# Four copies of the projected keys in a row, and four small VectorE steps at other places, in a fused attention and maxout kernel

## The chip, the core and the metric

The kernel runs on one core of a Trainium2 chip. A core has a matrix engine (TensorE, PE in the profile), a vector engine (VectorE, DVE), a scalar engine (ScalarE, ACT), GpSimd (POOL) and SyncE (SP). Each engine works through its own list of instructions in order. Semaphores make an instruction wait for results of another engine. DMA queues move data between the device memory and the on-chip memory (SBUF); TensorE writes its results to the banks of PSUM.

The metric is the device time of one execution in microseconds (us). For the kernel before it is 355.79 us, the median of three runs that lie between 355.75 and 355.89.

## The reference

```python
# attention with projected keys and values: 8 batches, 8 heads, 1024 positions, 64 wide, 64 projected rows
k_proj = np.einsum('ks,bhsd->bhkd', E, k)
v_proj = np.einsum('ks,bhsd->bhkd', F, v)
scores = scale * np.matmul(q, k_proj.transpose(0, 1, 3, 2))
scores = scores - np.max(scores, axis=-1, keepdims=True)
attn = np.exp(scores)
attn = attn / (np.sum(attn, axis=-1, keepdims=True) + 1e-09)
out = np.matmul(attn, v_proj)
# heads side by side: x has 8192 rows of 512
h1 = x @ w1          # 512 x 1024
h2 = x @ w2
g = np.maximum(h1, h2)
return g @ w_out     # 1024 x 512
```

## The kernel before

The kernel rewrites the second half. With the difference of the weights, wd = w1 - w2, the maximum of the two products is relu(x wd) + x w2. So the output is relu(x wd) w_out + x M, where M = w2 w_out is computed once. Both remaining products are done by Strassen's scheme in its form with seven block products: each takes sums and differences of blocks of x and g as one side (made by `step_s`, line 723) and differences of weight blocks as the other (`sub4`, line 614, kept in `T_sb`). Seven products are then combined by additions on VectorE (lines 778 and 885) and copies on ScalarE.

The work is cut into 16 *units*, two for each batch. A unit has up steps (x wd, `up_steps`) and down steps (the output product, `down_steps`). Each of them has seven products in the order 1, 2, 6, 5, 7, 3, 4. Products 1, 6, 5 and 7 are copied from PSUM to SBUF by ScalarE (`keep`, line 737, tile `p_sb`); for the up steps these copies are called s1, u1, s5 and u2. A later product accumulates into the same bank, so it has to wait for that copy: product 6 for s1, product 7 for u1, product 3 for s5, and product 4 for u2. The up products are on line 763, the down products on line 855.

The attention of a later batch is woven into these steps. For one batch its parts are:

- the keys' and values' projection (`step_kv_sets`, line 225) with its copies to SBUF
- the transposition of the projected keys (`step_kpt_sets`, line 254), and four ScalarE copies that set the result out in the tile `kpt`: one of 64x512 elements (line 262), one of 64x256 (line 263), and two of 64x128 (line 267)
- the queries' transposition, by PE with copies on VectorE or ScalarE in batch 1 (`step_qt`, lines 312 and 317), by DMA in batches from 2 on (line 324)
- the row maxima: PE multiplies queries and keys once (`step_top`, line 345), VectorE reduces the scores to their maxima (line 354, tile `top`), and PE transposes these (`step_topt`, line 366), so that ScalarE can copy them out (line 372)
- the scores less their maxima (line 386), the exponential, the sums and the values (line 401), and the division (line 462 or 517).

Nothing schedules this at run time. A list of *slots* gives the order of the up and down steps. A down product is cut into pieces, so that an attention step can stand between two pieces. The name `("U", n, h, i)` is the slot of an up product in the span of unit n's down steps, `("P", n, p, i)` is piece i of a down product, and `("G", n, h)` is a group of attention work. `at_slot(key, step, ...)` hangs a further step behind a slot. A step can return a function. The loop at the end of the kernel calls it after the next slot, and whatever that returns after the slot following:

```python
    pending = []
    for key, slot in slots:
        r = slot()
        pending = [g for g in [r, *(f() for f in pending)] if g is not None]
        for s in steps.pop(key, ()):
            r = s()
            if r is not None:
                pending.append(r)
```

This is how the keys' copies are spread. With `parts=2` the first two follow one slot after the transposition, and the last two one slot later, with that slot's own copies between them. In batches 3 to 7 the transposition hangs behind `("U", n, 0, 2)` (product 6), for odd n from 3 to 11. The next slot is the last piece of down product 2, and the one after is product 5, whose copy s5 so stands between the second and third copies of the keys.

Batch 1's attention is woven into unit 0's down steps, by a list of names with two slots to each down product. The number n counts the places in that list. At these places stand also the differences of weight blocks `step_t(1, ...)` (the part of `T_sb` made from `m_sb`, which holds M) and the four sums and differences of x for unit 1 (`sums_x` of `U[0, 1]`; S1 is made from S0, S3 from S1). In PE's order the names are: kk keys' projection, kv values' projection, qt queries' transposition, tp scores for the maxima, tt transposition of the maxima.

Of the kernel before, what the change touches and what calls it, by code (L numbers as in the profile page):

```python
# [16 lines left out]
def kernel(  # L17
# [41 lines left out]
    def mm_bank(dtype=FP32, n=None):  # L59
        if n is None:  # L60
            n = turn.pop(0)
            turn.append(n)
        return ps.tile([128, 512 if dtype == FP32 else 1024], dtype, tag=f"mm{n}", name="mm_ps")
# [150 lines left out]
    def step_kv_sets(t, bank=None, copy=nc.scalar.copy, which="kv"):  # L214
        late = bank is None
        if late:
            bank = att_banks()[:, 0, :]
        t["sets"] = True
        n = H // 2 * D
        for i, w in enumerate("kv"):  # L220
            if w not in which:
                continue
            for c in range(NC):
                for s in range(2):
                    nc.tensor.matmul(  # L225
                        out=bank[s * KP : (s + 1) * KP, i * n : (i + 1) * n],
                        lhsT=eft[i][:, c, :],
                        rhs=t[w][:, s * H // 2 : (s + 1) * H // 2, c, :],
                        start=(c == 0 and w == which[0]), stop=(c == NC - 1), skip_group_check=True,
                    )  # L230
        if "k" in which:
            kp = t["kp"] = proj.tile([128, H // 2 + 1, D], FP16, tag="kp", name="kp_sb")
            k_ps = bank[:, 0:n].rearrange("p (h d) -> p h d", d=D)
            copy(out=kp[:, 0 : H // 2, :], in_=k_ps)
            copy(out=kp[:, H // 2, :], in_=k_ps[:, 0, :])
            if which == "k":
                return

        def finish_v():
            vp, m = t["vp"], H // 2  # L240
            nc.vector.tensor_copy(
                out=vp[:, 0:m], in_=bank[:, n : 2 * n].rearrange("p (h d z) -> p h z d", d=D // 2, z=2)
            )
            for a, b in (0, KP), (KP, 0):
                nc.vector.tensor_copy(out=vp[a : a + KP, m:H], in_=vp[b : b + KP, 0:m])

        if late:
            return finish_v
        finish_v()
# [57 lines left out]
    def step_qt(t, h0, nh=2, i0=0, i1=NI, att=False, copy=nc.vector.tensor_copy):  # L307
        qt_ps = att_banks(FP16)[:, 0, :] if att else mm_bank(FP16)
        ni = i1 - i0
        for h in range(nh):  # L310
            for i in range(ni):
                nc.tensor.transpose(
                    out=qt_ps[:, (h * ni + i) * 128 : (h * ni + i + 1) * 128],
                    in_=t["q"][:, h0 + h, 2 * (i0 + i) : 2 * (i0 + i) + 2, :],
                    identity=ident16,
                )
        copy(
            out=t["qt"][:, h0 : h0 + nh, i0 * 128 : i1 * 128],
            in_=qt_ps[:, 0 : nh * ni * 128].rearrange("q (h n) -> q h n", h=nh),
        )  # L320
# [274 lines left out]
    U = {(b, o): {"n": n, "b": b, "o": o, "t": tiles[b]} for n, (b, o) in enumerate(units)}  # L595
# [376 lines left out]
    t = tiles[0]  # L972
# [118 lines left out]
    def at_slot(key, s, *a):  # L1091
        steps.setdefault(key, []).append(lambda: s(*a))
# [11 lines left out]
    t = tiles[1]  # L1104
    at_slot((0, 22), new_attn, t)
    at_slot((0, 22), lambda: turn.__setitem__(slice(None), [2, 3]))
    for n, x in enumerate((
        "", "kk", "qt00 qt10", "kpt", "qt01", "qt11 tp00", "tp10", "tt00", "kv tt10", "tp01", "tp11", "tt01",
        "tt11", "sc00", "sc10", "dn00 in00", "dn10 in10 at00", "AT10", "sc01",
    )):  # L1110
        key = ("P", n // 15, (n - 1) // 2 % 7, (n - 1) % 2) if n else (0, 22)
        for name in x.split():
            if name == "kk":
                at_slot(key, step_kv_sets, t, None, nc.vector.tensor_copy, "k")
                at_slot(key, loads, 2, "v")
            elif name == "kv":
                at_slot(key, step_kv_sets, t, None, nc.vector.tensor_copy, "v")
            elif name == "kpt":
                at_slot(key, step_kpt_sets, t, 0)
            else:  # L1120
                g, j = int(name[2]), int(name[3])
                s_ = {"qt": step_qt, "tp": step_top, "tt": step_topt, "sc": step_sc, "dn": step_dn,
                      "in": step_inv, "at": step_at, "AT": step_at}[name[:2]]
                args = (4 * g, 4, 2 * j, 2 * j + 2) if name[:2] == "qt" else (g, j)
                if name[:2] == "qt" and j == 0:
                    s_ = lambda *a: step_qt(*a, copy=nc.scalar.copy)
                at_slot(key, s_, t, *args, *([True] if name[:2] == "AT" else []))
        if n in (1, 4):
            at_slot(key, step_t, 1, (0, 1) if n == 1 else (2, 3))
        if 14 <= n < 18:  # L1130
            at_slot(key, step_tw, n - 14)
        if n == 5:
            at_slot(key, loads, 2, "q")
        if 2 <= n < 6:
            at_slot(key, sums_x, U[0, 1], ((2, 0, 1, 3)[n - 2],))


    t = tiles[2]
# [8 lines left out]
    for b in range(3, B):  # L1147
        t = tiles[b]
        n = 2 * b - 3
        key = ("U", n - 1, 1, 5)  # L1150
        at_slot(key, new_attn, t)
        at_slot(key, step_qt_dma, t, 0, H // 2)
        at_slot(key, step_qt_dma, t, H // 2, H)
        at_slot(("G", n, 0), lambda t=t: step_kv_sets(t, mm_bank(n=0), nc.vector.tensor_copy))
        at_slot(("U", n, 0, 2), step_kpt_sets, t)
        at_slot(("U", n, 0, 6), step_gate, t, "qt", H - 1)
        at_slot(("U", n, 0, 6), loads, b + 1, "k", "v", "q")
    for n, h in (3, 1), (4, 0), (4, 1), (5, 1), (6, 0), (6, 1), (7, 1), (8, 0):
# [3 lines left out]
    for i, (t, g, j) in enumerate(groups[1:]):  # L1162
        n, h = divmod(i + 1, 2)
# [8 lines left out]
    for i, (new, old) in enumerate(zip([*groups[1:], none], groups)):  # L1172
        n, h = divmod(i + 2, 2)
# [72 lines left out]
```

## Time and profile before

| what | value |
|---|---|
| median of three runs | 355.79 us |
| the profiled execution's own time | 355.79 us |
| its span, first to last instruction | 354.0 us |
| PE busy | 341.8 us, 97% of the span |
| VectorE busy | 276.0 us, 78% |
| ScalarE busy | 226.8 us, 64% |
| GpSimd busy | 38.9 us, 11% |
| granted TensorE clock | 1.00 |
| DMA, mean | 149 GB/s |

The profile shows one execution. A row of a timeline has the start, the duration, the engine, the line of the kernel, the operation, what it writes and reads, and how many such instructions in a row were put together. In square brackets is how long the engine sat idle before it, and what ended that. A row of the list of waits has who waited for whom, the total in us, how often, and the longest. Durations of neighbours on ScalarE and VectorE can overlap by a little, so the distance between two starts is read beside the duration.

### The profile page before, as it was taken

The numbers are of one execution on the slowest core, as the hardware profiler recorded it, in microseconds if no ns is written. First come the engines' busy times: TensorE is split into PE (matmuls) and PEld (weight loads), VectorE is DVE, ScalarE is ACT, GpSimd is POOL, SyncE is SP. The second block draws the span as 40 slices with busy tenths as digits, with TensorE's granted clock in tenths as the row PEclk, the third lists the DMA queues.
The fourth block names the chain that finished last, engine by engine and source line by source line (L and its number), as shares of the span: only waits on it lengthen the run. The fifth ranks groups of instructions, "written<-read, shape, count | busy, mean of one in ns | idle before, by whom it ended". The sixth has DMA issues, their size and how long they took to land.

```text
span 354.0 us, 11051 instructions
## 1 busy us (share of the span) xinstructions
PE 341.8 (97%) x4801; PEld 282.8 (80%) x4801; DVE 276.0 (78%) x513; ACT 226.8 (64%) x433; POOL 38.9 (11%) x58
## 2 busy tenths in 40 slices
PE   8889998999999999999999999999999999999996
PEld 3655587678888788888888788888888788888885
DVE  4776778886969789686969779686969879696773
ACT  2387653777675767666675767766675767676542
POOL 8375001020000300002000300002000000000000
PEclk9999999999999999999999999999999999999999
DMA  8999999999307999199976999199947511021223
GB/s 190 206 198 202 203 206 207 186 164 181 64 27 136 179 201 261 55 219 143 214 183 127 198 200 268 53 193 162 215 114 111 129 65 59 22 100 44 78 91 119
DMA packets 73712, 52.87 MB, mean 149 GB/s; under 512 B 26816, under 2 KB 73280, under 8 KB 73664
## 3 DMA queue, kind: packets, MB, share of 16 engines
q0 software_dynamic: 30688, 28.05, 50.3%
q1 hardware_dynamic: 42688, 23.93, 27.8%
q8 instruction: 37, 0.61, 0.7%
q10 hardware_dynamic: 288, 0.20, 0.2%
q14 instruction: 11, 0.09, 0.1%
HBM read 57.15 MB, written 16.78 MB: 209 GB/s over the span
## 4 chain that ended last, share of the span: by engine, by line
PE 69%; ACT 4%; DVE 4%; issue 0%; DVEq 0%
PE mm_ps L855 34%; PE mm_ps L763 21%; PE mm_ps L386 4%; PE att_ps L345 3%; PE mm_ps L225 3%; ACT p_sb L737 2%; PE att_ps L401 2%; DVE xt_sb L517 2%; ACT ex_sb L488 1%; DVE gt_sb L778 1%; PE att_ps L366 1%; ACT kpt L267 1%; DVE gt_sb L781 0%; DVE big L723 0%; DVE o_sb L953 0%
## 5 line engine op out<-in xcount | busy, mean ns | idle before, releaser
L737 ACT COPY p_sb<-mm_ps 128x512 f32<-128x512 f32 x179 | 101.7, 592 | 62.2 <-PE mm_ps L763 32.4
L855 PEld LDWEIGHTS <-big 128*128 128x128 f16 x768 | 72.3, 98 | 10.6 <-issue 3.2
L855 PE MATMUL mm_ps<-T_sb,big 128*128 128x256 f16 x576 | 77.3, 273 | 0.0
L778 DVE TENSOR_TENSOR gt_sb<-mm_ps,p_sb 128x512 f16<-128x512 f32 x56 | 38.5, 687 | 43.5 <-PE mm_ps L763 42.2
L763 PE MATMUL mm_ps<-big,big 128*128 128x256 f16 x336 | 50.4, 273 | 0.4 <-ACT p_sb L737 0.4
L763 PEld LDWEIGHTS <-big 128*128 128x128 f16 x448 | 43.8, 98 | 5.6 <-issue 0.6
L855 PE MATMUL mm_ps<-wo_sb,gt_sb 128*128 128x256 f16 x256 | 43.0, 273 | 0.0
L488 ACT ACTIVATE ex_sb<-mm_ps 128x512 f16<-128x512 f32 x50 | 27.1, 595 | 20.1 <-PE att_ps L401 11.4
L855 PEld LDWEIGHTS <-gt_sb 128*128 128x128 f16 x376 | 34.3, 98 | 6.9 <-issue 3.6
L354 DVE TENSOR_REDUCE top<-att_ps 128x8 f16<-128x512 f32 x56 | 36.0, 690 | 4.0 <-PE att_ps L345 4.0
L763 PEld LDWEIGHTS <-wd_sb 128*128 128x128 f16 x336 | 32.9, 98 | 3.8
L763 PE MATMUL mm_ps<-xt_sb,wd_sb 128*128 128x256 f16 x224 | 32.8, 273 | 0.0
L517 DVE TENSOR_TENSOR xt_sb<-att_ps,ld_sb 128x1024 f16<-128x1024 f32 x26 | 31.6, 1216 | 0.0
L885 DVE TENSOR_TENSOR o_sb<-mm_ps,p_sb 128x512 f32<-128x512 f32 x32 | 21.9, 683 | 4.1 <-ACT p_sb L914 2.0
L855 PE MATMUL mm_ps<-m_sb,xt_sb 128*128 128x256 f16 x128 | 24.4, 273 | 0.0
L304 POOL COPY junk<-qt_sb 1x1 f16<-1x1 f16 x6 | 1.7, 286 | 200.0 <-DMA qt_sb<-q_sb 200.0
L781 DVE TENSOR_SCALAR gt_sb<-gt_sb 128x512 f16<-128x512 f16 (+1 forms) x60 | 21.2, 354 | 2.1
L723 DVE TENSOR_TENSOR big<-gt_sb 128x1024 f16<-128x1024 f16 x32 | 21.9, 683 | 0.0
L855 PE MATMUL mm_ps<-wo_sb,big 128*128 128x256 f16 x128 | 21.5, 273 | 0.0
L345 PEld LDWEIGHTS <-qt_sb 128*128 128x128 f16 x256 | 16.6, 98 | 5.4 <-issue 4.2
L855 PE MATMUL mm_ps<-T_sb,gt_sb 128*128 128x256 f16 x120 | 20.3, 273 | 0.0
L855 PEld LDWEIGHTS <-xt_sb 128*128 128x128 f16 x188 | 18.2, 98 | 2.4 <-issue 0.2
(136 smaller groups left out, 554.4 us busy)
## 6 DMA issues: line engine op xcount, KB each, us to landing
out_dram<-o_sb SPq DMA_DIRECT2D x62, 256.0 KB, 2.6
k_sb<-in_k_dram POOLq DMA_DIRECT2D x7, 1024.0 KB, 9.9
v_sb<-in_v_dram POOLq DMA_DIRECT2D x7, 1024.0 KB, 13.8
q_sb<-in_q_dram POOLq DMA_DIRECT2D x5, 1024.0 KB, 20.9
q_sb<-in_q_dram POOLq DMA_DIRECT2D x6, 512.0 KB, 12.0
big<-in_moe_w_dram POOLq DMA_DIRECT2D x12, 128.0 KB, 6.5
v_sb<-in_v_dram POOLq DMA_DIRECT2D x4, 256.0 KB, 13.6
wo_sb<-in_moe_w_out_dram POOLq DMA_DIRECT2D x1, 1024.0 KB, 10.4
```

The lines of the kernel that those rows point to most:

```text
L345: nc.tensor.matmul(out=banks[i][:, h * 128 : (h + 1) * 128], lhsT=t["qt"][:, 4 * g + h, j * W + i * 128 : j * W + (i + 1) * 128], rhs=t["k ...
L354: nc.vector.tensor_reduce(out=top[k][:, i, :].rearrange("p (o h) -> p h o", o=2)[:, 0:4, :], in_=banks[i].rearrange("p (h o k) -> p h o k" ...
L386: nc.tensor.matmul(out=banks[e][pos : pos + Z, h * W : (h + 1) * W], lhsT=pick[rows, 2 * h + e, :] if shift else kpt_of(t, head, o)[:, s * ...
L488: nc.scalar.activation(out=t["ex", g, j][:, e, :], in_=banks[e], func=ACTF.Exp, scale=scale)
L517: nc.vector.tensor_tensor(out=x_out(t, g, j).rearrange("q z o n -> q o z n"), in0=at_ps.rearrange("q o (z n) -> q o z n", z=2), in1=ld[:, ...
L723: nc.vector.tensor_tensor(out=S(i), in0=S(0) if x is None else x, in1=y(), op=op)
L737: copy(out=x, in_=bank)
L763: nc.tensor.matmul(out=bank[:, m * W : (m + 1) * W], lhsT=w_[:, n_, (2 * d + m) * 128 : (2 * d + m + 1) * 128], rhs=a[:, n_, :], start=(n ...
L778: nc.vector.tensor_tensor(out=c_blk(j, c), in0=two(x), in1=two(y), op=ALU.add)
L781: nc.vector.tensor_scalar_max(ap, ap, 0.0)
L855: nc.tensor.matmul(out=bank[i][:, 0:CH] if two_banks else bank[:, i * CH : (i + 1) * CH], lhsT=a(c)[:, i * 128 : (i + 1) * 128], rhs=w_(c) ...
L885: nc.vector.tensor_tensor(out=o_sb, in0=two(x), in1=two(y), op=ALU.add)
```

## The change

Three things are set otherwise. No instruction is added or taken away.

- In batches 3 to 7, `step_kpt_sets` is called with `parts=1`: the four copies of the keys come one after the other, one slot after the transposition. The s5 copy comes behind them. Batch 2 keeps `parts=2`, and batch 1 had its four copies in a row before.
- In batch 1 the third and fourth weight differences (`step_t(1, (2, 3))`) go from place 4 to place 3.
- In batch 1, of the sums of x for unit 1, S0 goes from place 3 to place 2 (where S2 stands), S1 from place 4 to place 8 and S3 from place 5 to place 9. Between places 5 and 8 lie the first row maxima (tp00 and tp10).

```diff
-        if n in (1, 4):
-            at_slot(key, step_t, 1, (0, 1) if n == 1 else (2, 3))
+        if n in (1, 3):
+            at_slot(key, step_t, 1, (n - 1, n))
...
-        if 2 <= n < 6:
-            at_slot(key, sums_x, U[0, 1], ((2, 0, 1, 3)[n - 2],))
+        if n in (2, 8, 9):
+            at_slot(key, sums_x, U[0, 1], {2: (2, 0), 8: (1,), 9: (3,)}[n])
...
-        at_slot(("U", n, 0, 2), step_kpt_sets, t)
+        at_slot(("U", n, 0, 2), step_kpt_sets, t, 1)
```

On VectorE the stretch in question then has this order: T2 and T3 (line 614), the addition of line 885, both query copies (line 317), the four reductions (line 354), S1 (line 723), the values' three copies (lines 241 and 245), S3 (line 723), and the next reductions.

## The prediction

> **What bounds the kernel now.** I read the engine shares first, then the list of waits with TensorE as the one that waits, then the timelines around those waits.
>
> ```profile
> PE 341.8 (97%) x4801; PEld 282.8 (80%) x4801; DVE 276.0 (78%) x513; ACT 226.8 (64%) x433; POOL 38.9 (11%) x58
> ...
> PE 69%; ACT 4%; DVE 4%; issue 0%; DVEq 0%
> ```
>
> TensorE (PE) is busy for 97% of the span and holds 69% of the chain that ended last. Only what removes a pause of PE can shorten the run. The waits of PE (total us, times, longest) name the pauses that this change touches:
>
> ```profile
> PE att_ps L345 <- ACT kpt L267: 3.1, 5, 0.6
> ...
> PE att_ps L366 <- DVE top L354: 0.8, 1, 0.8
> ...
> PE att_ps L225 <- DVE top L354: 0.3, 1, 0.3
> ```
>
> The first row is one wait in each of batches 3 to 7. The other two stand in batch 1. The timeline of batch 3 (start us, duration, engine):
>
> ```profile
> 116.53 0.37 ACT L263 COPY kpt<-att_ps 64x256 f16<-64x256 f16 x1
> ...
> 116.79 0.60 PE L763 MATMUL mm_ps<-big,big 128*128 128x256 f16 x4
> ...
> 116.92 0.58 ACT L737 COPY p_sb<-mm_ps 128x512 f32<-128x512 f32 x1
> ...
> 117.40 0.68 DVE L723 TENSOR_TENSOR big<-gt_sb 128x1024 f16<-128x1024 f16 x1
> ...
> 117.53 0.42 ACT L267 COPY kpt<-att_ps 64x128 f16<-64x128 f16 x2
> 117.97 0.58 ACT L737 COPY p_sb<-mm_ps 128x512 f32<-128x512 f32 x1
> 118.00 0.61 PE L345 MATMUL att_ps<-kpt,qt_sb 128*128 128x128 f16 x8 [0.61 <-ACT kpt L267]
> ...
> 118.65 1.29 DVE L354 TENSOR_REDUCE top<-att_ps 128x8 f16<-128x512 f32 x2 [0.57 <-PE att_ps L345]
> ...
> 118.88 0.60 PE L763 MATMUL mm_ps<-big,wd_sb 128*128 128x256 f16 x4
> ```
>
> The reader is to see a copy of p_sb between the second keys' copy and the last two, and PE's score matmuls starting 0.05 us after the last two end. Batches 4 to 7 show the same rows (L345 at 158.02, 198.04, 238.06 and 278.08, idle 0.61 or 0.62). The timelines of VectorE (DVE), then of PE, in batch 1:
>
> ```profile
> 52.73 0.69 DVE L885 TENSOR_TENSOR o_sb<-mm_ps,p_sb 128x512 f32<-128x512 f32 x1 [1.23 <-ACT qt_sb L317]
> 53.34 0.68 DVE L317 COPY qt_sb<-mm_ps 128x1024 f16<-128x1024 f16 x1
> 53.94 0.41 DVE L614 TENSOR_TENSOR T_sb<-m_sb 128x512 f16<-128x512 f16 x1
> 54.27 0.42 DVE L614 TENSOR_TENSOR T_sb<-m_sb,T_sb 128x512 f16<-128x512 f16 x1
> 54.61 0.42 DVE L723 TENSOR_TENSOR big<-big,xt_sb 128x512 f16<-128x512 f16 x1
> 54.94 0.69 DVE L317 COPY qt_sb<-mm_ps 128x1024 f16<-128x1024 f16 x1
> 55.54 0.42 DVE L723 TENSOR_TENSOR big<-xt_sb,big 128x512 f16<-128x512 f16 x1
> 55.88 2.49 DVE L354 TENSOR_REDUCE top<-att_ps 128x8 f16<-128x512 f32 x4
> ```
>
> ```profile
> 55.56 0.82 PE L855 MATMUL mm_ps<-T_sb,big 128*128 128x256 f16 x6
> 57.22 0.29 PE L366 MATMUL att_ps<-ident,top 128*128 128x128 f16 x2 [0.85 <-DVE top L354]
> ...
> 58.42 1.06 PE L225 MATMUL att_ps<-v_sb,eft 128*64 128x256 f16 x16 [0.25 <-DVE top L354]
> ```
>
> DVE works without a gap from 52.73 to 58.37, and PE waits twice for what ends that stretch, the row maxima.
>
> **The change part by part.** No instruction is added or removed. The moved steps issue no DMA: as built, the orders on PE, GpSimd and SyncE, with their DMA issues, stay the same. ACT has five swaps and DVE one stretch in another order.
>
> *Keys' copies, five batches.* The two L267 copies move ahead of the p_sb copy (s5, product 5 of the up units). PE's pitch is 0.44 us for four matmuls (118.44 to 118.88), so from 116.79 it would reach L345 at 117.23; it started at 118.00 and lost 0.77. Now the copies: L263 starts at 116.53. Where L267 follows it directly, in batch 1, the starts are 53.13 and 53.40, 0.27 apart. So the pair runs from 116.80 to 117.22, and PE starts 0.05 later, at 117.27: 0.73 gained. If the pair could not overlap L263, it would start where the p_sb copy did, 116.92, which is 0.61 sooner than 117.53. If the wait vanished altogether, 0.77. Ends: 0.61 and 0.77; I take 0.73, from the same pair of instructions in the same order.
> The chain of waits puts DVE's L517 (ending 116.89) in front of the p_sb copy. I read that as a coincidence: in batch 2 the same copy stands 0.39 behind L263 too (78.04, 78.43), and L517 starts only at 78.45.
>
> What is late next: s5 waits behind the pair and starts 0.44 after the pair's start of 116.80 (117.53 to 117.97), so at 117.24, ending 117.82. Without overlap it ends at 117.94. Its bank is next written by product 3, L763 at 118.88, which moves up to 118.15: cover of 0.2 to 0.3. The next copy (u2) starts no later than before, and its bank's product 4 (119.75) comes at 119.02, against an end by 118.55. The reductions could start at 117.92 but stand behind L723 of 117.40; as 53.34 to 53.94 shows, a 0.68 row lets the next start after 0.60, so 118.00. They end at 119.29. PE loads their result at 120.08 now, 119.35 then: 0.06 of cover, no more. If L723 had to end first (118.08), PE would lose 0.03 to 0.06 of the 0.73. I take 0.72 per batch: 5 x 0.72 = 3.6, ends 5 x 0.61 = 3.05 and 5 x 0.77 = 3.85.
>
> The page "ScalarE: Activation LUTs" of the Trainium skill (section "What ACT_TABLE_LOAD costs") states that back-to-back activations overlap by about 93 ns. By it the copy taken out of PE's way would be worth 0.58 - 0.09 = 0.49, and the five batches 2.45. The trace disagrees: p_sb to L267 takes 0.61 (116.92 to 117.53), with no overlap.
>
> *Weight differences in batch 1.* The two T_sb differences (L614) go ahead of the L885 add. DVE stood idle 1.23 there, from 51.50 to 52.73; two rows of 0.41 and 0.42 fit, and their input m_sb is complete at 48.62 (the last L664 add, 47.94 for 0.68). L885 stays at 52.73, the first query copy at 53.34.
>
> *Two sums of x.* S0 only joins S2 (they ran back to back already). S1 and S3 leave the stretch before the maxima. The second query copy then needs only PE's transposes (53.56 + 0.61 = 54.17), so 54.22 with 0.05 of latency. The maxima follow 0.60 later, at 54.82: 1.06 sooner than 55.88. Their first pair is then ready for PE at 57.22 - 1.06 = 56.16. PE arrives at 55.56 + 6 x 0.11 = 56.22, so the first wait goes. Their last lets v's projection start at 58.42 - 1.06 = 57.36; PE arrives near 57.1, so a wait of about 0.25 stays, and PE is 1.06 ahead.
> S1 (0.42) now runs after the maxima, 57.31 to 57.73, in DVE's idle 1.16 ahead of L241 (59.52, then 58.46). S3 comes after the two L245 copies, which end at 60.44 - 1.06 = 59.38. It runs till 59.82, the next reduction could start at 59.74, and its scores are there at 60.84 - 1.06 = 59.78. The 0.40 of idle time is used up, for 0 to 0.04 of delay. Products that read S1 and S3 belong to unit 1's down steps, after 66 us. Taken: 1.04. Ends: 0.85 (only the first wait shown comes off) and 1.10 (0.85 + 0.25).
>
> [...]
>
> *Sum.* 3.60 + 1.04 = 4.64. After both places the later work follows PE: from 120 to 150 us PE has 30.00 busy us in 30. The profiled execution took 355.79 us (span 354.0 and 1.79 around it), equal to the median of the three runs. 355.79 - 4.64 = 351.15, say 351.1.
>
> **The rivals.**
> 1. *The maxima take the keys' place as the wait.* For it: the cover is 0.06 and DVE is packed from 109.9 to 118.1. Against it: L723 there waits for nothing of the swap. If half the gain per batch returned, 5 x 0.36 + 1.04 = 2.84: 353.0.
> 2. *Batch 1's lead is given back before 80 us.* For it: DVE already makes PE wait 0.20 at 71.66 (for L462), and ACT 0.39 at 79.07. Against it: both follow PE's own results, and batch 2's queries were transposed from 65.28 on, the last of them done at 72.05, 7 us ahead of the use at 79.40. The keys alone: 355.79 - 3.6 = 352.2.
> 3. *Slower: s5's copy holds product 3.* The swap puts s5 behind the pair, and product 3 writes the bank that s5 reads. It costs from an end of s5 at 118.15, and cancels a batch's gain from 118.88. With batch 1's 1.04 the run is slower only past 118.88 + 0.21. An end at 119.3 gives 5 x 0.42 - 1.04 = +1.1: 356.9. For it: in batch 2 PE does wait 0.39 for such a copy. Against it: the rows end s5 by 117.94.
> 4. *The wait isn't the keys'.* Then only batch 1 counts: 354.8. For it: L345 reads transposed queries too, and GpSimd's read of their second half comes at 117.31. Against it: its weight load, of queries, began at 117.12.
>
> **How the numbers follow.** Both parts as worked out: 0.77, between 350.8 (0.77 and 1.10) and 351.9 (0.61 and 0.85). Rival 1: 0.08. Rival 2: 0.08. Rival 3: 0.04. Rival 4: 0.03. The predicted time is that of the first. The range reaches to rival 2 and part of the way to rival 1, and 0.2 under the likeliest case's lower end, for the spread of the runs (355.75 to 355.89): 350.6 to 352.7. A measurement of this kernel tells about 0.2% (0.7 us) from no change. All cases but rival 3 are faster by more than that: 0.95; slower 0.04; same 0.01.
>
> **What the changed profile would show.** The row L345 <- L267 falls from 3.1 to under 0.3 us. The pair starts 0.27 after L263, and s5's copy follows it. Product 3 waits for nothing. In batch 1 the first maxima start near 54.8, L366 does not wait, L225 still waits about 0.25, and S3 ends just as the next reduction starts. A row of L763 waiting for p_sb five times, or L366 waiting for top five times, would prove me wrong, and so would PE back on its old times by 80 us.

## The result, and the profile after

| | before | after |
|---|---|---|
| median of four runs | 355.84 us (355.75 to 355.93) | 351.48 us (351.09 to 352.78) |
| ratio | | 0.9884 (95% interval 0.9857 to 0.991) |
| profiled execution, span | 355.79, 354.0 us | 351.74, 349.9 us |
| PE from batch 1's first L312 to the start of its last row of matmuls | 50.04 to 350.40: 300.36 us | 50.64 to 346.31: 295.67 us |

The kernel is 4.4 us faster by medians. The last row is the steadier measure, and most comparisons below use it: *PE's way* begins behind the run's first 50 us, where all kernels here have the same program. It became 4.69 us shorter. The profiled execution itself began late. The first wait for keys (L195) was 1.07 us in place of 0.22, and its first L312 stood 0.60 later. So 355.79 - 4.69 + 0.60 gives 351.70, against its 351.74.

The page's engine shares and its chain (the work that ended last, followed back from the last instruction), after:

```profile
PE 341.0 (97%) x4801; PEld 282.8 (81%) x4801; DVE 276.9 (79%) x513; ACT 225.8 (65%) x433; POOL 38.9 (11%) x58
...
PE 76%; DVE 0%; issue 0%; DVEq 0%
```

ScalarE has left the chain (4% before), VectorE's part fell from 4% to 0%, and PE holds 76% in place of 69%. PE's busy time has hardly changed (341.8 before); what went is pauses. The list of PE's waits, from 42 us on, now has these rows alone:

```profile
PE mm_ps L763 <- ACT p_sb L737: 0.3, 1, 0.3
PE att_ps L225 <- DVE top L354: 0.2, 1, 0.2
PE att_ps L401 <- DVE xt_sb L462: 0.2, 1, 0.2
```

The row L345 <- L267 of 3.1 us is gone, and so is L366 <- top of 0.8 us in batch 1. The timeline of batch 3, after:

```profile
116.07 0.37 ACT L263 COPY kpt<-att_ps 64x256 f16<-64x256 f16 x1
...
116.33 0.60 PE L763 MATMUL mm_ps<-big,big 128*128 128x256 f16 x4
116.34 0.43 ACT L267 COPY kpt<-att_ps 64x128 f16<-64x128 f16 x2
...
116.79 1.07 ACT L737 COPY p_sb<-mm_ps 128x512 f32<-128x512 f32 x2
116.82 0.61 PE L345 MATMUL att_ps<-kpt,qt_sb 128*128 128x128 f16 x8
116.94 0.68 DVE L723 TENSOR_TENSOR big<-gt_sb 128x1024 f16<-128x1024 f16 x1
...
117.54 1.29 DVE L354 TENSOR_REDUCE top<-att_ps 128x8 f16<-128x512 f32 x2
...
117.70 0.60 PE L763 MATMUL mm_ps<-big,wd_sb 128*128 128x256 f16 x4
```

The pair of L267 starts 0.27 behind L263. L345 starts 0.49 behind the L763 ahead of it, where it was 1.21 (116.79 to 118.00), so 0.72 came off. The pace without any wait is 0.44. The reduction starts 0.60 behind L723, and product 3 (the last row) waits for nothing. The timelines of VectorE, then of PE, in batch 1, after:

```profile
53.94 0.68 DVE L317 COPY qt_sb<-mm_ps 128x1024 f16<-128x1024 f16 x1
54.81 0.69 DVE L317 COPY qt_sb<-mm_ps 128x1024 f16<-128x1024 f16 x1 [0.19 <-PE mm_ps L312]
55.42 2.48 DVE L354 TENSOR_REDUCE top<-att_ps 128x8 f16<-128x512 f32 x4
57.81 0.42 DVE L723 TENSOR_TENSOR big<-big,xt_sb 128x512 f16<-128x512 f16 x1
59.06 0.42 DVE L241 CAST vp_sb<-att_ps 128x256 f16<-128x256 f32 x1 [0.84 <-PE att_ps L225]
59.52 0.46 DVE L245 COPY vp_sb<-vp_sb 64x256 f16<-64x256 f16 x2
60.00 0.42 DVE L723 TENSOR_TENSOR big<-xt_sb,big 128x512 f16<-128x512 f16 x1
60.38 2.49 DVE L354 TENSOR_REDUCE top<-att_ps 128x8 f16<-128x512 f32 x4
```

```profile
56.82 0.28 PE L366 MATMUL att_ps<-ident,top 128*128 128x128 f16 x2
...
57.96 1.06 PE L225 MATMUL att_ps<-v_sb,eft 128*64 128x256 f16 x16 [0.21 <-DVE top L354]
```

This clock is 0.60 late, so the maxima's 55.42 is 54.82 on the old one. The second query copy waits for PE's transposes (0.19) and no longer for VectorE's own queue. L366 doesn't wait. L225 still waits, 0.21. S3 (60.00) just fits in front of the next reductions, which start 0.04 behind the end of PE's scores (59.73 + 0.61).

### The profile page after: what moved, and what is told of

It reads as the page before. It is cut to its first block, busy times and chain, and to the rows that moved or that the text cites. A ratio compares the mean times of both kernels' runs of the same rounds, so it can differ in the third digit from the quotient of the medians.

```text
span 349.9 us, 11052 instructions
## 1 busy us (share of the span) xinstructions
PE 341.0 (97%) x4801; PEld 282.8 (81%) x4801; DVE 276.9 (79%) x513; ACT 225.8 (65%) x433; POOL 38.9 (11%) x58
## 4 chain that ended last, share of the span: by engine, by line
PE 76%; DVE 0%; issue 0%; DVEq 0%
PE mm_ps L855 38%; PE mm_ps L763 24%; PE mm_ps L386 4%; PE att_ps L345 3%; PE mm_ps L225 3%; PE att_ps L401 3%; PE att_ps L366 1%; PE att_ps L254 0%; DVE o_sb L953 0%; PE mm_ps L947 0%; DVEq L953 0%
## 5 line engine op out<-in xcount | busy, mean ns | idle before, releaser
L737 ACT COPY p_sb<-mm_ps 128x512 f32<-128x512 f32 x179 | 101.2, 592 | 58.7 <-PE mm_ps L763 32.5
L763 PE MATMUL mm_ps<-big,big 128*128 128x256 f16 x336 | 50.4, 273 | 0.3 <-ACT p_sb L737 0.3
L763 PEld LDWEIGHTS <-big 128*128 128x128 f16 x448 | 43.8, 98 | 5.7 <-issue 0.5
L763 PEld LDWEIGHTS <-wd_sb 128*128 128x128 f16 x336 | 32.9, 98 | 3.8
L763 PE MATMUL mm_ps<-xt_sb,wd_sb 128*128 128x256 f16 x224 | 32.8, 273 | 0.0
L723 DVE TENSOR_TENSOR big<-gt_sb 128x1024 f16<-128x1024 f16 x32 | 21.9, 683 | 0.0
L824 ACT ACTIVATE gt_sb<-mm_ps 128x512 f16<-128x512 f32 x28 | 17.0, 607 | 4.6 <-PE mm_ps L763 4.6
```

The source lines that it names most:

```text
L723: nc.vector.tensor_tensor(out=S(i), in0=S(0) if x is None else x, in1=y(), op=op)
L737: copy(out=x, in_=bank)
L763: nc.tensor.matmul(out=bank[:, m * W : (m + 1) * W], lhsT=w_[:, n_, (2 * d + m) * 128 : (2 * d + m + 1) * 128], rhs=a[:, n_, :], start=(n ...
L824: nc.scalar.activation(out=out, in_=in_, func=ACTF.Relu)
```

## The experiments

Each was made to tell one step of the prediction from a rival.

**The keys' copies alone, and batch 1's moves alone.** The first kernel keeps only the third hunk of the diff, the second only the other two.

```diff
-        at_slot(("U", n, 0, 2), step_kpt_sets, t)
+        at_slot(("U", n, 0, 2), step_kpt_sets, t, 1)
```

> Edit: only the keys' four copies in a row in batches 3 to 7; batch 1 as before. My theory (each of the five waits of L345 for L267 is worth 0.73 us, and batch 1's part 1.05 by itself): 355.8 - 5 x 0.73 = 352.2; no row L345 <- L267; batch 1 keeps its waits of 0.85 and 0.25 for the row maxima. Rival (the two parts help each other, PE loses what one part wins alone): 353 or more, with a new PE wait in batches 3 to 7.

> Edit: only batch 1's two moves; the keys' copies split as before. My theory: 355.8 - 1.05 = 354.8; PE's way from the queries' first transposition of batch 1 (L312, 16 at once) to the first scores (L386) takes 13.10 us in place of 14.16; the five waits of 0.61 for L267 stay. Rival (batch 1's lead is given back before 80 us): 355.8, and the way from the first L312 to the first L345 of batch 2 is as long as before, 29.48 us.

The keys alone: median 352.32 us beside 355.88 (ratio 0.9898, 0.9873 to 0.9922), PE's way 296.69, which is 3.67 shorter, or 5 x 0.73. Batch 1 alone: 354.97 (0.998, 0.9958 to 1.0002), way 299.27, 1.09 shorter; from L312 to the first L386 it took 13.10 (before 14.16), and to batch 2's first L345 28.41 (before 29.48). Its ratio's interval holds 1, so its gain rests on the trace and not on the times. PE's waits in this second kernel still show the keys' row as before:

```profile
PE att_ps L345 <- ACT kpt L267: 3.1, 5, 0.6
```

The two gains, 3.67 and 1.09, make 4.76, and both together gave 4.69. So the parts don't help or hinder each other, and the lead of batch 1 is kept to the end. Rivals 2 and 4 of the prediction fall.

**The two halves of batch 1's part.** One kernel puts the weight differences back, the other the sums of x.

```diff
-        if n in (1, 3):
-            at_slot(key, step_t, 1, (n - 1, n))
+        if n in (1, 4):
+            at_slot(key, step_t, 1, (0, 1) if n == 1 else (2, 3))
```

```diff
-        if n in (2, 8, 9):
-            at_slot(key, sums_x, U[0, 1], {2: (2, 0), 8: (1,), 9: (3,)}[n])
+        if 2 <= n < 6:
+            at_slot(key, sums_x, U[0, 1], ((2, 0, 1, 3)[n - 2],))
```

> Edit: the changed kernel with the two weight differences back at their old place (between the two query copies); the sums of x stay behind the maxima. My theory: the differences hold the second query copy back to 53.34 + 0.60 + 2 x 0.33 = 54.60 on the old kernel's clock, so the maxima start 0.67 sooner than before, not 1.06: PE's way from the first L312 of batch 1 to the first L386 takes 13.49 (before 14.16, both moves 13.10), and L366 waits about 0.2 for the maxima. Rival (the sums alone are the gain, the differences add nothing): 13.10.

> Edit: the changed kernel with the sums of x back at their old places (S1 and S3 ahead of the maxima); the weight differences stay ahead of the L885 add. My theory: S1 ends the first query copy's wait for 0.33 and S3 stands between the second and the maxima for another 0.34, so the maxima start about 0.66 sooner than before, and the way from L312 to L386 takes 13.50; the two halves (0.67 and 0.66) don't add up to 1.33 but to 1.06, since with both the query copy waits for PE's own transposes. Rival (the differences alone are the gain): 13.10.

The way from L312 to L386 took 13.49 and 13.48 us. In both, PE waited again for the first maxima. PE's row in the kernel with the sums alone moved:

```profile
56.85 0.28 PE L366 MATMUL att_ps<-ident,top 128*128 128x128 f16 x2 [0.17 <-DVE top L354]
```

Each half is worth about 0.67, and both 1.06. The second half of the gain is cut off by PE's transposes, as the 0.19 of idle time ahead of the second query copy shows above.

**How much cover s5 has.** Cover is the time between the end of s5's copy and product 3's write to the same bank. One more copy stands between the keys' last and s5's.

```diff
             rest()
+            if parts == 1:
+                nc.scalar.copy(out=spare, in_=ones16)
```

> Edit: the changed kernel, with one more ScalarE copy (128x512, from a constant to a tile that nobody reads) between the keys' last copy and s5's copy, in batches 3 to 7. The cover that I worked out for s5 is tested: in the changed kernel s5 ends at about 117.33 and product 3 writes its bank at 117.70. My theory: the extra copy takes 0.5 to 0.6, so product 3 waits 0.15 to 0.3 in each of five batches, the row L763 <- p_sb appears five times more, and the time rises by 0.8 to 1.5 over the changed kernel's, to 352.0 to 353.0. Rival (s5's bank is not what binds, or the cover is wider than 0.35): no wait of L763 beyond the one of batch 2, and the time stays at 351.1 to 351.7.

PE's waits, its timeline in batch 3, and ScalarE's (the edit moved the line numbers by three: L766 is L763, L740 the p_sb copy; L274 is the extra copy):

```profile
PE mm_ps L766 <- ACT p_sb L740: 1.3, 6, 0.3
```

```profile
117.24 0.60 PE L858 MATMUL mm_ps<-T_sb,big 128*128 128x256 f16 x4
118.05 0.60 PE L766 MATMUL mm_ps<-big,wd_sb 128*128 128x256 f16 x4 [0.21 <-ACT p_sb L740]
```

```profile
116.77 0.62 ACT L274 COPY spare<-ones 128x512 f16<-128x512 f16 x1
117.41 1.07 ACT L740 COPY p_sb<-mm_ps 128x512 f32<-128x512 f32 x2
```

The wait came in each of the five batches, so the mechanism of rival 3 is real, and the change stays clear of it by its cover. The size was missed. The median is 353.15 us, above the 352.0 to 353.0 expected, and PE's way is 297.47, 1.80 longer than the changed kernel's. I had added up the idle time that a row shows, 0.21, but the matmuls start 0.81 apart in place of 0.44: 0.37 in each batch, and 5 x 0.37 = 1.85. The idle time is counted from a matmul's end, which lies about 0.16 behind the moment at which the next could have started. The extra copy took 0.62 and held s5 back by 0.64; less the 0.37 that product 3 lost, that leaves a cover of 0.27.

**The same row of copies in batch 2.** There they stand ahead of u1's copy.

```diff
-    at_slot(("U", 1, 0, 1), step_kpt_sets, t)
+    at_slot(("U", 1, 0, 1), step_kpt_sets, t, 1)
```

> Edit: the changed kernel, with the four copies in a row in batch 2 too (there they stand ahead of u1's copy, which PE's product 7 waits for). My theory (a copy pushed behind the keys' pair costs as soon as PE needs its bank): u1's copy starts 0.27 + 0.44 - 0.39 = 0.32 later against L263, so the one wait of L763 for p_sb grows from 0.31 to about 0.63, and the time from about 351.3 to 351.6. Rival (a row of copies is good wherever it stands): the wait stays at 0.3 or goes.

PE's timeline around that product 7:

```profile
77.76 0.60 PE L855 MATMUL mm_ps<-T_sb,big 128*128 128x256 f16 x4
79.08 0.60 PE L763 MATMUL mm_ps<-big,big 128*128 128x256 f16 x4 [0.72 <-ACT p_sb L737]
```

The wait grew to 0.72, a little more than the 0.63 expected. Counted from batch 1's first L312, product 7 starts 0.33 later than in the changed kernel (28.30 against 27.97), as expected, and PE's way is 295.96, 0.29 longer. (The one time, 352.14, says little.) A row of four copies is good only where what it pushes back has cover.

**Batch 2 in another order.** The keys' copies start right behind their transposition, and down product 6's copy goes behind u1's.

```diff
-    at_slot(("U", 1, 0, 1), step_kpt_sets, t)
+    at_slot(("U", 1, 0, 1), step_kpt_sets, t, 0)
...
-            st["u1"] = keep("pd", whole(6, "X", None))
+            bank = whole(6, "X", None)
+            if u["n"] == 1:
+                return lambda: st.__setitem__("u1", keep("pd", bank))
+            st["u1"] = keep("pd", bank)
```

> Edit: the changed kernel, and in batch 2 the keys' four copies start right behind their transposition (no slot later), with the copy of down product 6 put behind u1's. My theory: ScalarE is idle there for 0.84 us, which the keys' copies then use; they end by 77.4 (in the changed kernel's time), u1 by 78.0, and the one wait of L763 for p_sb (0.31 us idle, 0.47 of PE's pace) goes, with none for the keys in its place: 0.4 us faster than the changed kernel, 350.7 to 351.1 by median. Rival (the down copy put behind then holds PE): a new wait of L855 for p_sb near 80 us, and no gain.

VectorE and PE there:

```profile
78.23 1.21 DVE L517 TENSOR_TENSOR xt_sb<-att_ps,ld_sb 128x1024 f16<-128x1024 f32 x1
79.36 1.28 DVE L354 TENSOR_REDUCE top<-att_ps 128x8 f16<-128x512 f32 x2
```

```profile
80.69 0.23 PE L366 MATMUL att_ps<-ident,top 128*128 128x128 f16 x1 [0.37 <-DVE top L354]
```

The wait of L763 went (the way from L312 to batch 2's first L345 fell from 28.42 to 27.85), but neither theory had what came next. VectorE's queue held the maxima, PE waited 0.37 for them, and only 0.23 of the 0.57 was left at the end (295.44). This is the mechanism of the prediction's rival 1, at another batch. The median, 351.14, just misses the 350.7 to 351.1 expected and lies within the changed kernel's spread on that chip (351.32; 351.04 to 351.84):

> The changed kernel as it is, beside the others on their chip. From five waits of 0.73 and batch 1's 1.05: 351.1 where the first load of keys lets PE start on time (L195 waits 0.2 as in the profile of before), and up to 1 us more where it comes late; PE's way from the first L312 of batch 1 to its last matmul stays within 0.1 of the first profile's whatever the start.

Its profile gave a way of 295.62, 0.05 from the first, from a start at 50.21.

**One sum less ahead of those maxima.** The sum of g that stood there goes behind them.

```diff
-            for key, i in (end, 0), (one, 1), (("P", n, 1, m), 2), (("P", n, 2, m), 3):
+            for key, i in (end, 0), (one, 1), (("P", n, 1, m), 2), (("U", 1, 0, 5) if n == 1 else ("P", n, 2, m), 3):
```

> Edit: the kernel with batch 2's copies in the other order (the run before this one), and there one sum of g (S3 of unit 1, line 723, 0.68 us) behind the row maxima instead of ahead of them. My theory: in the run before, PE's wait for u1 gave way to a wait of 0.37 for the maxima, because VectorE's stretch ahead of them was full; with the sum gone from it the maxima start with PE's scores, 0.4 sooner, and the wait falls under 0.1. PE's way from batch 1's first L312 to batch 3's first L345 falls to 65.6 (changed kernel 66.18, the run before 65.99), and the time to about 0.5 under the changed kernel's, 350.7 by median. Rival (the way from 80 us on is bound elsewhere): 65.99 again.

```profile
78.61 1.30 DVE L354 TENSOR_REDUCE top<-att_ps 128x8 f16<-128x512 f32 x2 [0.53 <-PE att_ps L345]
```

VectorE now waits for PE here. The way to batch 3's first L345 is 65.61 as expected, and the whole way 295.10, 0.57 under the changed kernel's. Its median on that chip, 351.44 beside 356.41 (ratio 0.986, 0.9837 to 0.9883), can't show so little, and misses the 350.7. So both kernels ran on one chip:

> The changed kernel, on one chip with the next. From its earlier profiles: PE's way from batch 1's first L312 to batch 3's first L345 66.18 us; 351.1 to 351.7 by median.

> The kernel with batch 2's copies and one sum of g in the other order, on one chip with the changed kernel. My theory: 0.57 us less than the changed kernel by PE's way (65.61 against 66.18), so a median 0.4 to 0.7 lower, 350.5 to 351.2. Rival: the start of the run, which differs by up to 1 us between executions, covers it, and the medians lie within 0.3.

Medians 351.85 (a little above its 351.1 to 351.7) and 351.14; against the kernel before 0.9885 (0.9846 to 0.9923) and 0.9846 (0.9821 to 0.987). The difference of 0.7 has the expected sign, but the intervals overlap; the ways, 295.66 and 295.10, differ by 0.56, as in the run before. I take this version for faster by about 0.56 us on the trace's word, not on that of the times.

**What sets the distance of ScalarE's copies.** L262 goes from first to last of the four.

```diff
-            nc.scalar.copy(out=dst[lo, 0], in_=src[lo])
+            if parts != 1:
+                nc.scalar.copy(out=dst[lo, 0], in_=src[lo])
             nc.scalar.copy(out=dst[hi, 1, :, 1], in_=src[hi, :, 0])
...
             rest()
+            if parts == 1:
+                nc.scalar.copy(out=dst[lo, 0], in_=src[lo])
```

> Edit: the changed kernel, with the first of the four copies (L262, partitions 0 to 63) put last, in batches 3 to 7: the order is 64 to 127 three times, then 0 to 63. It tests what sets the distance of ScalarE's copies. My theory (two neighbours overlap by about 0.1 us only when both start at the same partition): u1 to the first keys' copy 0.59 with no overlap (0.49 in the changed kernel), last L267 to the copy of partitions 0 to 63 again without overlap, and from that copy to s5's 0.49 with overlap. The four copies then end 0.1 later, and L345 waits up to 0.1 in each batch, 0 to 0.5 in all. Rival (what sets the distance is a change of the PSUM tile that is read): u1 to the first keys' copy and the keys' last copy to s5 both without overlap, the copies among themselves with it.

ScalarE in batch 3, first in the changed kernel, then with this edit (L264, L268 and L740 are the old L263, L267 and L737; L274 is the moved copy):

```profile
114.44 0.63 ACT L513 ACTIVATE ld_sb<-ld_sb 128x512 f32<-128x512 f32 x1
114.99 0.58 ACT L737 COPY p_sb<-mm_ps 128x512 f32<-128x512 f32 x1
115.48 0.58 ACT L262 COPY kpt<-att_ps 64x512 f16<-64x512 f16 x1
```

```profile
115.39 0.59 ACT L740 COPY p_sb<-mm_ps 128x512 f32<-128x512 f32 x1
116.00 0.37 ACT L264 COPY kpt<-att_ps 64x256 f16<-64x256 f16 x1
116.27 0.43 ACT L268 COPY kpt<-att_ps 64x128 f16<-64x128 f16 x2
116.71 0.58 ACT L274 COPY kpt<-att_ps 64x512 f16<-64x512 f16 x1
117.19 1.06 ACT L740 COPY p_sb<-mm_ps 128x512 f32<-128x512 f32 x2
```

u1 to the first keys' copy is 0.61, with no overlap (0.49 in the changed kernel, 114.99 to 115.48). The pair to L274 is 0.44 for 0.43: no overlap, though both read one PSUM tile. From L274 to s5 it is 0.48 for a copy of 0.58, so these two overlap, though they read different PSUM tiles. The rival fails at both of these distances. PE's way is 296.30, 0.63 longer, or 0.13 in each batch, a little above the 0 to 0.5 expected; the single time, 352.74, also holds the latest start seen (first L312 at 51.04).

## Why the prediction was right

Measured were 351.48 us, in the range given. By steps:

- **The keys' copies, 0.73 in each batch.** Shown by the run with them alone, 3.67 in five batches. The distance of 0.27 from L263 to the pair, taken from batch 1, held.
- **What is late next.** s5's cover of 0.2 to 0.3 came out at about 0.3 (117.70 against an end near 117.37; 0.27 by the extra copy). The reduction started 0.60 behind L723, and L366 did not wait for it.
- **Weight differences and sums, 1.04 together.** PE gained 1.06 to the first L386. S3's delay of 0 to 0.04 didn't come: the reductions start 0.04 behind PE, as they did before. The remaining wait of L225, forecast at 0.25, was 0.21.
- **The sum, 4.64.** PE's way: 4.69, 4.74 and 4.70 in the changed kernel's three profiles.
- **The bubble's two prices.** That a copy taken out is worth its 0.61 and not less, since the copy and the pair start at different partitions, agrees with the order test. The Trainium skill's page "ScalarE: Activation LUTs" (section "What ACT_TABLE_LOAD costs") states, without a condition, that back-to-back activations overlap by about 93 ns. The copies here that read PSUM overlap by 0.10 where both start at the same partition and not at all where the start changes (0.61 from s5 to the pair), so here the measurement decides.

Two readings of the prediction were off, without harm. Against rival 2 it took 72.05 for the time at which batch 2's queries were done. That is the end of SyncE's row; the profile puts 7.8 us between this transposition's issue (68.57) and its landing, so they were there at about 76.4, 3 us ahead of their use and not 7. And the stretch of VectorE called packed from 109.9 to 118.1 holds one idle time of 0.22, ahead of 114.39.

What was not forecast is the start. The first profile's execution took 351.74, and what it took beyond the forecast doesn't lie in the steps: its start was 0.60 late. For the other three of the first four runs, and so for the 0.4 us between the forecast and their median, that is likely but not shown, since they have no profile.

Rival 1 didn't happen in batches 3 to 7. That such a wait can take back a gain is shown in batch 2, where the maxima took the place of a wait removed.

## What to carry to other kernels

When an engine that holds the chain waits for the last of several small copies, the cheapest cure can be the order on the other engine; the most that the swap can be worth is the pace lost, start to start, which is about 0.16 us more for each wait than the idle time shown here (0.77 for 0.61, of which 0.73 was gained). For each step pushed back, look up who reads it next and when: 0.3 us of cover made the same row of copies a gain in five batches, and no cover made it a loss in a sixth. After each wait removed, ask what the queue of the next engine holds, since the next wait can take most of the gain.

## What the runs showed of the hardware

- **ScalarE's copies from PSUM overlap by about 0.1 us where both start at the same partition, and not where the start changes between 0 and 64.** Starts of 0.27 for a copy of 0.37 (both from 64 on), 0.49 for 0.58 (both from 0 on), but 0.59 for 0.58, 0.39 for 0.37 and 0.61 for 0.59 where the start changes between 0 and 64. The order test moved one such distance each way. In these copies the side read and the side written start alike, so which of them counts isn't shown. The same start is not always enough: in the kernel with the extra copy, that copy (0.62, from 0 on, but read from SBUF) and s5's behind it (from 0 on, read from PSUM) start 0.64 apart in all five batches. The change from SBUF to PSUM alone isn't the reason, since L513, which reads SBUF, and the u1 copy behind it overlap by 0.08 (114.44, 0.63 long, to 114.99). The last copy before s5's that read PSUM started at 64, and it may be this start that counts; no run tests it.
- **The start of a run varies by a microsecond.** Batch 1's first L312 stood at 50.02 to 51.04 us in fourteen profiles of kernels with the same program for the first 50 us, with the first wait of L195 for keys between 0 and 1.75 us. Two profiles waited about the same there and yet stood 0.76 apart (0.33 and 50.02; 0.34 and 50.78, in the kernels with batch 1's moves alone and with batch 2's row), so that wait isn't all of it. Their L195 already starts 0.58 apart (7.59 and 8.17); why, stays open.
